# Strassen-Winograd on quarters for the token gating of a fused attention, token-mixing and gating kernel

## The chip, the cores and the metric

One core of a Trainium2 chip. The time is device microseconds of one execution of the whole program, from its first to its last instruction and what lies around them. The kernel before was run three times.

## The reference

Three blocks follow each other, all float32, with B = 2 batches, S = 768 tokens, 8 heads of 64, so D = 512 features:

```python
x = attention(q, k, v)            # near keys of a window, 24 block summaries
theta = x @ w_theta               # 512x512
y = einsum('ts,bsd->btd', w_tok_r, x*cos(theta)) + einsum(..., w_tok_i, x*sin(theta))
u = x + y;  x = u + relu(u @ w_ch)
h = gelu(x @ w_in)                # 512 -> 1024
u, v = h[..., :512], h[..., 512:]
v_n = (v - mean) / sqrt(var + 1e-6) * g_ln
v_s = einsum('ts,bsd->btd', w_sg, v_n) + b_sg[None, :, None]   # token gating, 768x768 by 768x512
out = x + (u * v_s) @ w_out
```

The change is about the line `v_s`: for each batch a product of w_sg (768 x 768) with the normalized v (768 x 512).

## The kernel before

**Number format.** Each float32 product is three matmuls of rounded halves (`mm3`, L347): both operands are split into a high half (a copy to fp32r, on ACT or POOL, `copy`, L337 and L339) and a low half (source minus high, on DVE or POOL, `diff`, L345); TensorE then adds high by high (L350), high by low (L351) and low by high (L352) in PSUM. Weights are split too (`unit`, `unit_f32`, `high_low`).

**Stages.** *Attention* (to about 82 us): pairs of heads, loads k, vT, q, v; scores S, their maximum m and P = S - m on DVE (L640, L646), exp on ACT (L654), transposes PT, copies Pt (ACT or DVE), O, the norm x = O/sum on DVE (L684 to L688), transposes X, copies xT. *Mixing*: theta (th), kk and rr (its turns), f (cos and sin on ACT, L771 and L772, times x), z (split f), y and ys (the two mixing products with w_r, w_i, w_ri). *ch*: u and u @ w_ch. *in_v* (L879): iv groups of 12 matmuls of 512 columns, gelu to vf, statistics st (BN_STATS and aggregate, L902), then for the batch the root (L908), reciprocal rv (L910), six norms (L925), and the splits vh, vl into vn. *in_u* (L945): iu groups, gelu to ut. *sg* (L966): for each batch, four blocks of 128 features by two pieces of tokens (512 and 256): 6 tiles of tokens x 3 matmuls with the split v_n as stationary operand and the split w_sg as moving operand; then the gate (x g_ln + b_sg, DVE, L984), times u (L996), and the split of the result into g for the next product. *outp* (L1016): 12 matmuls for each of 4 blocks of features and 3 blocks of 512 tokens (the last one in two of 256), evacuation with + x on DVE (L1034), store (L1042).

**What sets the order.** The program describes each step as an `op` with its engines, estimated durations, predecessors, buffers, and a key; a list scheduler in the file (`Order`, `play`, L143) picks by key and fixes the order of every engine, of SP's DMA issues too, before the program is built. The tables PLAN, LEAD and SHIFT are numbers that shift these keys. At run time each engine works through its list in that order; SP is one queue for all DMAs. Buffers are slots: 27 W (1024 columns), 19 H (512), 4 X (1536), 6 PSUM banks B and one double bank S. The main order of the keys behind the mixing:

```python
for step, k in ((ch, 0), (ch, 1), (ch, 2), (in_v, 0), (in_u, 0), (in_u, 1), (sg, 0), (in_v, 1),
                (in_u, 2), (outp, 0), (sg, 1), (outp, 1), (outp, 2)):
```

w_sg comes as nine units (`unit_f32`, L473): load, high, low, kept in W slots until sg of batch 1.

## Time and profile before

| what | value |
|---|---|
| runs | 381.68, 382.77, 384.49 us (median 382.77) |
| the profiled execution | 382.36 us |
| its span, first to last instruction | 379.8 us |
| mean granted TensorE clock | 1.000 |
| busy: PE, weight loads, DVE, ACT, POOL | 372.7, 314.9, 241.0, 179.8, 87.5 us |
| matmuls | 2983 |
| DMA | 40.84 MB |

Busy is the time in which an engine had an instruction under way; a matmul's end is modelled, and neighbours overlap, so its step is read from two starts in the timeline. A releaser is what ended an idle time. An idle engine that is not the bound costs nothing.

### The profile page before, as it was taken

The page shows a single profiled execution, that of the slowest core. Times are in us where ns is not written, and L with a number is a line of the kernel's source. Part 1 is how long each engine was busy: PE and PEld are TensorE (multiplying, and loading weights), DVE is VectorE, ACT ScalarE, POOL GpSimd, SP SyncE. Part 2 cuts the span into 40 slices and gives each one's busy share as a digit, 9 for nine tenths or more (in the row PEclk, how much of TensorE's full clock was granted, in tenths as well). Part 3 has the DMA queues.
Part 4 walks back from the last instruction along what each step waited for, and adds up shares of the span by engine and source line. Part 5 has one row for each costly group of instructions (what it writes and reads, how often), then busy time and mean ns, then how long its engine had stood idle before and what let it go on. Part 6 is the DMA issues. An engine that isn't in the chain of part 4 may idle for free.

```text
span 379.8 us, 7439 instructions
## 1 busy us (share of the span) xinstructions
PE 372.7 (98%) x2983; PEld 314.9 (83%) x2983; DVE 241.0 (63%) x418; ACT 179.8 (47%) x321; POOL 87.5 (23%) x113
## 2 busy tenths in 40 slices
PE   8899999999999999999999999999999999999996
PEld 4787887888888888888888888888888889889885
DVE  4999998978786746337869557370344485246422
ACT  2787899969764832225657226362311351012100
POOL 6556546464400200003304403000000030000000
PEclk9999999999999999999999999999999999999999
DMA  8999899980040000013696010010000000200022
GB/s 269 347 361 285 281 296 333 315 286 1 3 151 14 2 0 2 0 28 115 217 340 217 13 44 0 0 36 7 0 2 0 1 2 28 85 0 0 29 93 100
DMA packets 18257, 40.84 MB, mean 108 GB/s; under 512 B 2416, under 2 KB 8752, under 8 KB 18224
## 3 DMA queue, kind: packets, MB, share of 16 engines
q1 hardware_dynamic: 18224, 40.38, 32.0%
q8 instruction: 23, 0.38, 0.4%
q14 instruction: 10, 0.08, 0.1%
HBM read 36.92 MB, written 3.15 MB: 106 GB/s over the span
## 4 chain that ended last, share of the span: by engine, by line
PE 92%; DMA 3%; DVE 2%; issue 1%; SPq 1%; ACT 0%; DVEq 0%
PE y L350 6%; PE y L351 6%; PE y L352 6%; PE sg L351 4%; PE sg L350 4%; PE sg L352 4%; PE ys L351 3%; DMA k<-in_kT_dram 3%; PE ys L352 3%; PE ys L350 3%; PE th L350 3%; PE ch L350 3%; PE ch L351 3%; PE iu L351 3%; PE iu L350 3%; PE iv L351 3%
## 5 line engine op out<-in xcount | busy, mean ns | idle before, releaser
L337 ACT ACTIVATE g<-gf 128x256 fp32r<-128x256 f32 (+1 forms) x20 | 9.1, 462 | 50.8 <-DVE gf L996 43.1
L345 DVE TENSOR_TENSOR z<-f,z 128x512 fp32r<-128x512 f32 x20 | 14.3, 715 | 21.9 <-ACT z L337 19.9
L352 PE MATMUL ys<-w_ri,z 128*128 128x256 f32 x96 | 27.1, 282 | 0.0
L351 PE MATMUL ys<-w_ri,z 128*128 128x256 f32 x96 | 27.1, 282 | 0.0
L350 PE MATMUL ys<-w_ri,z 128*128 128x256 f32 x96 | 26.7, 278 | 0.0
L337 ACT ACTIVATE z<-f 128x512 fp32r<-128x512 f32 x20 | 12.6, 630 | 27.7 <-PE ys L352 19.9
L902 DVE BATCH_NORM_STATS2 st<-vf 128x6 f32<-128x512 f32 x12 | 8.3, 693 | 25.1 <-ACT vf L893 25.1
L350 PEld LDWEIGHTS ys<-w_ri,z 128*128 128x128 f32 x96 | 18.0, 188 | 4.4
L351 PEld LDWEIGHTS ys<-w_ri,z 128*128 128x128 f32 x96 | 18.0, 188 | 3.8
L984 DVE SCALAR_TENSOR_TENSOR gf<-sg,g_sb,bsg 128x512 f32<-128x512 f32 (+1 forms) x16 | 9.9, 617 | 16.8 <-PE sg L352 16.7
L350 PE MATMUL th<-w_th,xh 128*128 128x512 f32 x48 | 19.8, 413 | 0.0
L350 PE MATMUL y<-w_i,z 128*128 128x512 f32 x48 | 19.3, 401 | 0.0
L350 PE MATMUL y<-w_r,z 128*128 128x512 f32 x48 | 19.2, 401 | 0.0
L351 PE MATMUL y<-w_r,z 128*128 128x512 f32 x48 | 19.1, 397 | 0.0
L351 PE MATMUL y<-w_i,z 128*128 128x512 f32 x48 | 19.0, 395 | 0.0
L352 PE MATMUL th<-w_th,xh 128*128 128x512 f32 x48 | 18.8, 392 | 0.0
L351 PE MATMUL th<-w_th,xh 128*128 128x512 f32 x48 | 18.8, 391 | 0.0
L350 PE MATMUL ch<-u,w_ch 128*128 128x512 f32 x48 | 18.7, 390 | 0.0
L351 PE MATMUL ch<-u,w_ch 128*128 128x512 f32 x48 | 18.7, 390 | 0.0
L352 PE MATMUL y<-w_r,z 128*128 128x512 f32 x48 | 18.7, 389 | 0.0
L352 PE MATMUL y<-w_i,z 128*128 128x512 f32 x48 | 18.7, 389 | 0.0
L352 PE MATMUL ch<-u,w_ch 128*128 128x512 f32 x48 | 18.7, 389 | 0.0
(294 smaller groups left out, 1133.1 us busy)
## 6 DMA issues: line engine op xcount, KB each, us to landing
v<-in_vW_dram SPq DMA_DIRECT2D x16, 193.5 KB, 5.3
k<-in_kT_dram SPq DMA_DIRECT2D x8, 384.0 KB, 5.0
q<-in_qT_dram SPq DMA_DIRECT2D x16, 192.0 KB, 5.4
vT<-in_vT_dram SPq DMA_DIRECT2D x8, 384.0 KB, 5.6
w_r<-in_w_rT_dram SPq DMA_DIRECT2D x6, 511.8 KB, 5.9
w_i<-in_w_iT_dram SPq DMA_DIRECT2D x6, 511.8 KB, 6.9
w_th<-in_w_theta_dram SPq DMA_DIRECT2D x4, 511.8 KB, 6.1
w_ch<-in_w_ch_dram SPq DMA_DIRECT2D x4, 511.8 KB, 4.4
```

The source lines that it names most:

```text
L337: ACT.activation(dst, src, AF.Copy, scale=scale)
L345: EN[e].tensor_tensor(out=lo, in0=src, in1=hi.bitcast(F32), op=ALU.subtract)
L350: PE.matmul(ps, ah, bh, start=first, stop=False, skip_group_check=True)
L351: PE.matmul(ps, ah, bl, start=False, stop=False, skip_group_check=True)
L352: PE.matmul(ps, al, bh, start=False, stop=last, skip_group_check=True)
L902: DVE.bn_stats(out=st, in_=T(f"vf{b}_{i}")[:])
L984: DVE.scalar_tensor_tensor(out=T(gn)[:, :n], in0=T(bk)[:, :n], scalar=g_sb[:, f:f + 1], in1=T("bsg")[:, o:o + n], op0=ALU.mult, op1=ALU.add)
```

## The change

The token gating of a batch is now done by Strassen and Winograd's seven products of quarters. Token and feature halves give quarters A11, A12, A21, A22 of the normalized v (3 tiles of 128 tokens by 256 features each) and B11 to B22 of w_sg (3 tiles by 384 columns). `values` makes the sums of A for both batches (four adds of 768 columns, Qa, Qt) and splits seven operands (Qh, Ql, each 768 wide). `weights` does the same for each of three tiles of w_sg: four loads (Qw, 128 x 384), four sums (Qb), seven splits (Qy..h, Qy..l, 384 wide); these are written to a DRAM scratch (dQx, op Qz, two writes of 192 KB) and later read back (Qx, 384 KB) and copied in place on ACT or POOL. `sg` runs products 1, 6, 2, 7, 5, 3, 4, each for two batches and two blocks of features: 9 matmuls of 384 columns in a bank Qs. Product 2 adds into product 1's bank and 3 into 5's; the other sums (U, R) are made by ACT (product 1's copy) and DVE (Qe). Then Qn (gate), Qm (times u), Qg and Qk (split) for 16 blocks of 384 tokens. The norm of v is its own step (`ln`) and runs on ACT or DVE. The output goes in blocks of 384 tokens, the last one in two of 192. The numbers in PLAN and LEAD are new and SHIFT holds an offset for almost every op, so that the order of all engines differs from the start. TensorE's sg matmuls go from 144 of 512 and 144 of 256 columns to 252 of 384; the output's from 132 of 512 and 24 of 256 to 180 of 384 and 24 of 192; filler matmuls (L410) from 13 to 9. Table loads on ACT go from 9 to 13. DMA instructions go from 139 to 208 rows.

```diff
-    at0=-2.908, at0_pair=5.41, at0_half=1.015, at1=29.379, at1_pair=12.053, at1_half=-11.199,
+    q_from=121.281, q_step=28.693, q_back=223.53, at0=-10.9, at0_pair=7.346, at0_half=2.395,
...
+    dr = ctx.enter_context(tc.tile_pool(name="dr", bufs=1, space=bass.MemoryType.DRAM))
...
-    for c in range(NT):
-        unit_f32(("sg", c), [rows(w_sgT, c)[:, :512]], 170 + 3 * c)
-    for c in range(3):
-        unit_f32(("sgs", c), [rows(w_sgT, 2 * c + i)[:, 512:] for i in range(2)], 190 + 3 * c)
...
+            op(f"vo{b}_{i}", {"ACT": act(512), "DVE": 0.54}, norm, after=[f"rv{b}"], use=[vx],
...
+        l1 = hl(1, "A11", n0, [x0])
+        add("c", "t", "A11", "A21", True, n0, [x0], [(t, "W")])
+        add("b", "A11", "A22", "t", True, [l1, f"Qa{b}c"] + n1, [x0, x1, t])
+        hl(6, "A11", [f"Qa{b}b"], [x0])
+        l2 = hl(2, "A12", n1, [x1])
+        add("d", "A12", "A12", "A11", True, [l2, f"Qa{b}b"], [x0, x1])
+        hl(7, "t", [f"Qa{b}c"], [t])
+        add("a", "A21", "A21", "A22", False, n1 + [f"Qa{b}c"], [x0, x1])
+        hl(5, "A21", [f"Qa{b}a"], [x0])
+        hl(3, "A12", [f"Qa{b}d"], [x1])
+        hl(4, "A22", n1, [x1])
...
+            def aside(e):
+                made["d" + nm] = dr.tile([P, QS], F32, tag="d" + nm, name="d" + nm)
+                for i, y in enumerate((h, l)):
+                    nc.sync.dma_start(made["d" + nm][:, sl(i, 384)], T(y)[:, :384].bitcast(F32))
+            op(f"Qz{k}{p}", {"SP": 0.86}, aside, after=[l], use=[h, l], size=2 * moved(P, 1536), parts=2)
+            op(nm, {"SP": 0.43},
+               lambda e: nc.sync.dma_start(T(nm, F32R)[:, :QS].bitcast(F32), made["d" + nm][:]),
+               after=[f"Qz{k}{p}"], new=[(nm, "W")], size=moved(P, 3072), early=PLAN["q_back"],
+               spare=PLAN["q_spare"])
+            op(nm + "l", copies(QS, ("ACT", "POOL")),
+               lambda e: copy(e, T(nm, F32R)[:, :QS], T(nm)[:, :QS].bitcast(F32)), after=[nm],
+               use=[nm], port=("POOL",))
...
+        for p in (1, 6, 2, 7, 5, 3, 4):
+            for b in range(B):
+                for j in range(2):
...
+                    def mm(e, bk=bk, c0=c0, start=start, h=h, l=l, ws=ws, j=j):
+                        for k in range(3):
+                            s = slice(256 * k + 128 * j, 256 * k + 128 * j + 128)
+                            w = T(ws[k], F32R)
+                            mm3(T(bk)[:, c0:c0 + 384], (T(h, F32R)[:, s], T(l, F32R)[:, s]),
+                                (w[:, :384], w[:, 384:768]), start and k == 0, k == 2)
...
-    for step, k in ((ch, 0), (ch, 1), (ch, 2), (in_v, 0), (in_u, 0), (in_u, 1), (sg, 0), (in_v, 1),
-                    (in_u, 2), (outp, 0), (sg, 1), (outp, 1), (outp, 2)):
+    for step, k in ((ch, 0), (ch, 1), (ch, 2), (in_v, range(4)), (in_u, 0), (in_v, range(4, 8)), (in_u, 1),
+                    (in_v, range(8, 12)), (in_u, 2)):
         t = step(k, t)
+    for b in range(B):
+        ln(b)
+    t = sg(t)
+    for k in ((0, 1), (1, 1), (0, 0), (1, 0)):
+        t = outp(k, t)
```

**Order, DVE, end of in_v of batch 1.** Lines of the changed file lie 300 to 460 higher. Before, from the last statistics on:

```order
L902 BN_STATS st1_5_3610<-vf1_5_3606 128x6
L903 BN_AGGR mv1_3406<-st1_5_3610 128x2
L910 RECIPROCAL rs1_3407<-rs1_3407 128x6
L925 TENSOR_SCALAR vf1_0_3404<-vf1_0_3404,mv1_3406,rs1_3407 128x512
L925 TENSOR_SCALAR vf1_1_3431<-vf1_1_3431,mv1_3406,rs1_3407 128x512
```

In the changed kernel (Ql11 is the low half of operand 1 of batch 1, Qt1 a difference of quarters, Ql07 batch 0's):

```order
L1191 BN_STATS st1_5_3685<-vx1_1_3607 128x6
L1192 BN_AGGR mv1_3483<-st1_5_3685 128x2
L1205 RECIPROCAL rs1_3484<-rs1_3484 128x6
L1206 SCALAR_TENSOR_TENSOR rs1_3484<-mv1_3483,rs1_3484 128x6
L1218 TENSOR_SCALAR vx1_0_3478<-vx1_0_3478,mv1_3483,rs1_3484 128x512 x3
L1261 TENSOR_TENSOR Qt1_3722<-vx1_0_3478 128x768
L645 TENSOR_TENSOR Ql11_3746<-vx1_0_3478,Qh11_3728 128x768
L1261 TENSOR_TENSOR vx1_0_3478<-vx1_1_3607,Qt1_3722 128x3x256
L645 TENSOR_TENSOR Ql07_3762<-Qt0_3480,Qh07_3732 128x768
```

Three of the six norms moved to ACT, and sums of quarters and their low halves stand where the plain splits stood; Ql11 is the low half that product 1 of batch 1 reads.

**Order, ACT, attention stage.** Before (one pair of table loads up to here; kk, f: theta's turns and the sine, P: exp):

```order
L763 ACTIVATE f0_0_1293<-rr0_1283 128x256
L337 ACTIVATE Pt5_0_0_1301<-PT5_0_0_1287 120x384
L337 ACTIVATE Pt5_0_1_1313<-PT5_0_1_1297 120x384
L771 ACT_TABLE_LOAD
L771 ACTIVATE f0_0_1293<-f0_0_1293,half_pi_134 128x256
L772 ACTIVATE f0_0_1293<-rr0_1283 128x256
L654 ACT_TABLE_LOAD
L654 ACTIVATE P6_1_1321<-P6_1_1321 128x720
```

In the changed kernel:

```order
L1054 ACT_TABLE_LOAD
L1054 ACTIVATE f0_0_1042<-f0_0_1042,half_pi_136 128x256
L1055 ACTIVATE f0_0_1042<-rr0_1024 128x256
L937 ACT_TABLE_LOAD
L937 ACTIVATE P4_1_1064<-P4_1_1064 128x720
L1026 ACTIVATE kk2_1141<-th2_1050 128x512
L1046 ACTIVATE f1_0_1147<-rr1_1054 128x256
L1054 ACT_TABLE_LOAD
L1054 ACTIVATE f1_0_1147<-f1_0_1147,half_pi_136 128x256
L1055 ACTIVATE f1_0_1147<-rr1_1054 128x256
```

f of tile 0 has moved ahead by some ten rows, f of tile 1 stands two rows behind P of the next pair, and each return to P is a further table load.

**Order, SP, loads of w_in.** Before (w_inu, w_inv: the halves of w_in; w_sg..r: the raw gating weights):

```order
L448 DMA w_inu0_2664<-in_w_in_dram 128x2047
L479 DMA w_sg3r_2689<-in_w_sgT_dram 128x512
L448 DMA w_inu1_2708<-in_w_in_dram 128x2047
L479 DMA w_sg4r_2713<-in_w_sgT_dram 128x512
L479 DMA w_sg5r_2743<-in_w_sgT_dram 128x512
L448 DMA w_inu2_2753<-in_w_in_dram 128x2047
L448 DMA w_inu3_2757<-in_w_in_dram 128x2047
L448 DMA w_inv0_2784<-in_w_in_dram 128x2047
L448 DMA w_inv1_2795<-in_w_in_dram 128x2047
```

In the changed kernel:

```order
L1321 DMA dQx12_2746<-Qy12h_2713 128x384
L1321 DMA dQx12_2746<-Qy12l_2732 128x384
L1321 DMA dQx23_2793<-Qy23h_2721 128x384
L1321 DMA dQx23_2793<-Qy23l_2790 128x384
L1294 DMA Qw200_2803<-in_w_sgT_dram 128x384
L1294 DMA Qw210_2828<-in_w_sgT_dram 128x384
L1321 DMA dQx21_2841<-Qy21h_2830 128x384
L1321 DMA dQx21_2841<-Qy21l_2838 128x384
L1321 DMA dQx22_2864<-Qy22h_2859 128x384
L1321 DMA dQx22_2864<-Qy22l_2862 128x384
L748 DMA w_inu2_2887<-in_w_in_dram 128x2047
L748 DMA w_inv2_2890<-in_w_in_dram 128x2047
```

The loads of the gating weights now carry writes of their splits with them, each behind a split by ACT, DVE or POOL, and these stand ahead of w_inu2 and w_inv2; three earlier w_inu loads and four more pairs of writes stand above this piece.

## Rows read from the trace of the kernel before

**Rows 1.** The page: busy time of each engine, last chain, one group of weight loads.

```profile
PE 372.7 (98%) x2983; PEld 314.9 (83%) x2983; DVE 241.0 (63%) x418; ACT 179.8 (47%) x321; POOL 87.5 (23%) x113
...
PE 92%; DMA 3%; DVE 2%; issue 1%; SPq 1%; ACT 0%; DVEq 0%
...
L350 PEld LDWEIGHTS ys<-w_ri,z 128*128 128x128 f32 x96 | 18.0, 188 | 4.4
```

**Rows 2.** Windows of 20 us: us, busy us (instructions) by engine, PEclk, DMA share, GB/s.

```profile
0.00:20.00 20.00, 17.45 (x375) 12.14 (x375) 14.09 (x25) 10.40 (x17) 12.90 (x35) 1.00 0.94 308
20.00:40.00 20.00, 18.87 (x426) 15.78 (x423) 19.18 (x35) 16.25 (x29) 10.65 (x15) 1.00 0.97 316
40.00:60.00 20.00, 20.00 (x410) 16.74 (x403) 19.03 (x39) 18.40 (x33) 12.07 (x18) 1.00 0.92 301
60.00:80.00 20.00, 19.55 (x258) 16.37 (x258) 15.48 (x29) 17.71 (x33) 12.21 (x11) 1.00 0.97 323
...
100.00:120.00 20.00, 20.00 (x107) 17.15 (x106) 14.81 (x23) 14.12 (x28) 3.05 (x2) 1.00 0.22 79
...
200.00:220.00 20.00, 20.00 (x90) 16.49 (x89) 15.98 (x28) 9.77 (x16) 7.55 (x5) 1.00 0.38 120
...
300.00:320.00 20.00, 20.00 (x118) 17.78 (x117) 12.88 (x24) 8.06 (x13) 3.48 (x4) 1.00 0.04 14
```

**Rows 3.** Timeline of PE: start us, duration us, engine, line, operation.

```profile
335.62 0.39 PE L352 MATMUL sg<-w_sg,vn 128*128 128x512 f32 x1
...
340.83 0.39 PE L351 MATMUL sg<-w_sg,vn 128*128 128x512 f32 x1
...
346.05 0.28 PE L350 MATMUL sg<-w_sgs,vn 128*128 128x256 f32 x1
...
354.56 0.28 PE L352 MATMUL sg<-w_sgs,vn 128*128 128x256 f32 x1
...
376.50 0.28 PE L352 MATMUL o_3b<-g,w_out 128*128 128x256 f32 x1
```

**Rows 4.** Instructions by form, PE, 195 to 380 us: xcount | busy us, mean ns.

```profile
L350 PE MATMUL sg<-w_sg,vn 128*128 128x512 f32 x48 | 18.7, 389 | 0.0
...
L350 PE MATMUL o<-g,w_out 128*128 128x512 f32 x44 | 17.1, 390 | 0.0
...
L350 PE MATMUL sg<-w_sgs,vn 128*128 128x256 f32 x48 | 13.6, 283 | 0.0
```

**Rows 5.** One line of DVE (ns min/median/max, first and last start), then instructions by form.

```profile
L688 DVE TENSOR_TENSOR x<-O,ri x16: 557/558/558, 15.9 to 81.6; 128x384 f32<-128x384 f32 x16
...
L345 DVE TENSOR_TENSOR w_ch<-w_ch3r,w_ch 128x512 fp32r<-128x512 f32 x1 | 1.8, 1796 | 0.0
...
L432 DVE SCALAR_TENSOR_TENSOR w_th<-w_th1r,w_th 128x512 fp32r<-128x512 f32 x1 | 0.7, 693 | 0.0
```

**Rows 6.** Instructions by form, ACT.

```profile
L337 ACT ACTIVATE Pt<-PT 120x384 f32<-120x384 f32 x26 | 11.5, 490 | 5.0 <-PE PT L659 4.8
...
L337 ACT ACTIVATE v<-ones 24x774 f32<-24x774 f32 x10 | 8.5, 851 | 0.3
...
L908 ACT ACT_TABLE_LOAD x2 | 2.6, 1283 | 0.0
```

**Rows 7.** Instructions by form, POOL.

```profile
L345 POOL TENSOR_TENSOR xh<-xT,xh 128x384 fp32r<-128x384 f32 x8 | 8.1, 1010 | 1.5 <-ACT xh L337 1.4
```

**Rows 8.** Timeline of ACT around the square root of batch 1.

```profile
302.84 1.28 ACT L908 ACT_TABLE_LOAD   x1
304.14 0.30 ACT L908 ACTIVATE rs<-mv,eps_t 128x6 f32<-128x6 f32 x1
304.98 1.28 ACT L957 ACT_TABLE_LOAD   x1 [0.54 <-issue]
```

**Rows 9.** DMA issues: xcount, KB each, median us to landing.

```profile
k<-in_kT_dram SPq DMA_DIRECT2D x8, 384.0 KB, 5.0
```

**Rows 10.** Timeline of DVE, the last output piece.

```profile
376.82 0.42 DVE L1034 TENSOR_TENSOR o_3bs<-o_3b,xT 128x256 f32<-128x256 f32 x1 [1.01 <-PE o_3b L352]
```

## The prediction

> **What bounds the kernel now.** I read the busy times and the chain that ended last first [rows 1]. TensorE is busy 372.7 of 379.8 us and the chain is 92% TensorE; DVE has 63%, ACT 47%, POOL 23%. Then the stretches of 20 us [rows 2]: from 80 to 360 us every stretch, those not shown too, reads 20.00 for PE, so no joint between stages costs anything there. TensorE has holes only in the attention stage: 17.45, 18.87, 20.00 and 19.55 of 20 up to 80 us, where DVE has 19.18 and 19.03 in the second and third and the DMA share is 0.92 to 0.97. [...] So a matmul saved behind 80 us is worth its whole step, as long as the other engines keep feeding PE, and work added to DVE or ACT before 80 us can cost.

> A matmul's step is the distance of two starts: its busy time (389 or 283 ns, [rows 4]) has a modelled end and overlaps the next. Of 24 sg matmuls of 512 columns in a row the first starts at 335.62 and the last at 340.83: 5.21/23 = 0.2265 us each (by groups of 12, 2.72, I use 0.2267). Of 72 with 256 columns the first starts at 346.05 and the last at 354.56: 8.51/71 = 0.1199 [rows 3]. The line through both has 0.1068 us for 256 columns more, so 0.1733 us for 384 columns and 0.0933 for 192.

> **The change part by part.** Products: sg was 144 matmuls of 512 and 144 of 256 columns [rows 4], 144 x (0.2267 + 0.1199) = 49.9 us. Now it is 7 products x 4 (two batches, two halves of features) x 9 = 252 of 384 columns, 252 x 0.1733 = 43.7 us: **-6.2 us**. An eighth of the columns goes; a little is given back since the fixed part of a step is paid on shorter ones.

> Output: 132 x 0.2267 + 24 x 0.1199 = 32.8 us becomes 180 x 0.1733 + 24 x 0.0933 = 33.4 us: **+0.7 us**. Both are behind 80 us, where PE is the bound: **-5.5 us**.

> The step of 384 is interpolated. A 256-column step of 0.12 is already shorter than the busy time of a weight load (188 ns, [rows 1]), so loads overlap and don't set the step. [...]

> Weights: seven splits of each of 3 k-tiles come in place of nine f32 units. That is 12 sums and 21 high and 21 low halves of 384 columns, spread over 100 to 290 us, where DVE has 4 to 15 us idle in every 20, ACT 6 to 15 and POOL 12 to 19 (the fullest, 100:120 and 200:220, are shown [rows 2]). By 558 ns for a 384-wide DVE instruction, 490 ns on ACT and 1010 ns for a POOL difference [rows 5 to 7], it is some 30 us over three engines: hidden. The scratch is 42 writes of 192 KB and 21 reads of 384 KB, 16 MB; DMA's share is 0 to 0.38 in every stretch of 100 to 180 and 200 to 320, so the bytes are hidden. What is not free is order: SP issues one after another, and the write of a low half that is not ready holds the loads behind it. In the order, w_inu's last tile and all of w_inv stand behind eight such pairs. By adding durations, PE asks for that w_inu tile some 3.5 us later than it can be there. Nothing, then; without that cover each us is paid one to one.

> Normalization of batch 1: before, sg of batch 1 began long after its statistics, with sg of batch 0 and o0 between. Now the first product needs it at once. After the last iv group PE has only three iu groups of 2.72 and the two batch-0 halves of product 1 (18 x 0.1733 = 3.12), 11.3 us. The chain in that time: gelu, BN_STATS and aggregate, table load 1.28, sqrt 0.30, reciprocal [rows 8], three norms of 0.6, Qt's difference 0.95, table load back, two gelus, Qh11's 768-wide copy 0.85, Ql11's difference 0.95. The last gelu waits for the third iu group, so the chain's end is fixed by PE itself. An evacuation starts 0.32 us behind the last matmul's start (376.50 and 376.82, [rows 3, 10]), 0.42 for 512 columns; then 0.60, 0.85 and 0.95 make 2.8 us. The third matmul of batch 1, which first uses Ql11, starts 0.23 + 3.12 + 0.35 = 3.7 us behind it. Hand-offs take some of the 0.9 left; I take **+0.2 us** for a row ahead in line that is late, with 0 and 2 as bounds.

> Within sg: DVE has some 65 instructions, 37.5 of 44 us; ACT about 25, POOL about 20. Product by product the feeding halves have 1.5 to 6 us of slack. Nothing, in the likely case.

> Attention stage: the new numbers move every engine's order from the start. Up to the last norm (L688; last at 81.6 us, [rows 5]) DVE has 4.5 us more: two Pt copies 1.1, two xh splits 2.1, one vs reduce 0.94, one f product 0.7 and one more weight sum 0.7, less one z difference 0.7 and a small copy. ACT has four more table loads (1.283 us each [rows 6]; 13 in place of 9 in the whole kernel) and 9.1 us more up to the last Pt copy, 66.3 in place of 57.2. Against this, four of thirteen filler matmuls are gone, and 1.05 us of mixing leaves the stretch. Bounds: -1 us (fewer holes), +4.5 us (all of DVE's extra is paid, since 19 of 20 us are busy at 20 to 60). I take **+1.0 us**: nearer the low end, as PE itself has only 1.6 us of holes between 20 and 80 us [rows 2] and DVE 6.3 us. [...]

> Tail: the last block is 192 columns, its evacuation 0.15 us shorter than the 0.42 of [rows 10]: -0.1 at most, left out.

> **Sum:** the profiled execution took 382.36 us (span 379.8 and 2.6 around it): 382.4 - 5.5 + 0.2 + 1.0 = **378.0 us**. It lies 0.4 below the median of 382.77, well inside the runs' 381.7 to 384.5.

> **Rivals.** *A: the helpers bind in sg, no change.* POOL has two- and one-input work of 20 us beside DVE's 37.5, and DVE is 85% full. With POOL beside it, a 512-wide DVE difference went from 693 to 1796 ns [rows 5]. If ten of DVE's two-input instructions meet POOL at +1.1 us, 11 us go into 6.5 us of room: 4.5 us of waiting products, 382.5. For it: these rows, and that POOL had only 0 to 3.5 us of work per 20 from 260 us on. Against: POOL's tasks there number 20, some while DVE reads PSUM. [...]

> *B: the attention stage gives most of it back.* If DVE's 4.5 us is paid whole: 378.0 - 1.0 + 4.5 = 381.5, no change. For: DVE 19 of 20 us. Against: PE can take theta and mixing groups meanwhile, and their sum is the same.

> *C: the read-back comes late, slower.* A product needs three reads of 384 KB into W slots and three copies in place. A 384 KB load took 5.0 us to landing [rows 9], and the next two are on the queue behind it, by 300 GB/s another 1.3 us each; with the 0.85 us copy, 8.5 us from a slot that comes free, while one product covers 36 x 0.1733 = 6.2 us. If slots come free only one product ahead, each of five later products waits 2.2 us: 378.0 + 11 = 389. It decides where fewer than one and a half products' slots (five of the 27) are free ahead. For: SP's order has the last 17 reads in a run, most of them behind a wait for PE, and ACT copies nearly all. Against: w_inu and w_inv leave eight slots as sg starts. A fall of the clock would add to it; none shows before.

> *D: a 384-column step is not between its neighbours* but bound by loads, 0.188: 252 x 0.188 + 180 x 0.188 + 2.2 = 83.4 against 82.7 us before: 384.5 with the rest, no change. Against it: the 0.12 step.

> **How the numbers follow.** About 1% is what a measurement of this kernel can tell from no change: 378.9 to 386.6. Chances: forecast 0.55 (374.5 to 380.5, four fifths of it below 378.9 as the attention term is the only wide one), A 0.15, B 0.15, C 0.12, D 0.03. Faster: 0.55 x 0.8 + some of A and B = 0.50; slower: C and part of A = 0.14; the rest 0.36. The range takes in the bounds (382.4 - 5.5 - 1 - an unmodelled 1 below; A, B and half of what is between them and C above): 374.5 to 386.

> **What would show it.** Right: matmuls of sg start 0.173 apart, 252 of them; PE at 20.00 in all stretches from 85 us on; the last L688 norm (L971 there) by about 83 us; PE idle under 0.5 us before the batch-1 half of product 1. Wrong: PE idle before Qs groups with DVE (A) or ACT's copies of Qx and the DMA of Qx (C) as releaser; PE holes over 5 us before 85 us (B); a step of 0.18 or more (D); the granted clock under 1.00.

## The result: 0.99 of the time before

The changed kernel took 380.84 us (median of 20 runs), the kernel before 384.40 beside it: ratio 0.9906, 95% interval 0.9882 to 0.993. The ratio leaves out the few runs far above the rest (383.99 and 928.91 us of the changed kernel, 2096.41 of the kernel before). The forecast was 378.0 with 374.5 to 386. The profiled execution took 380.85 us with a span of 379.1; that of before 382.36 with 379.8. So the two traces explain 1.5 us, 0.7 in the span and 0.8 around it. The medians differ by 3.6: the profiled execution of before is one of its short ones.

The page of the changed kernel has the busy times, the last chain, one group of the products, and the queue that carries instructions:

```profile
PE 369.4 (97%) x2991; PEld 321.9 (85%) x2991; DVE 261.6 (69%) x453; ACT 204.1 (54%) x349; POOL 120.1 (32%) x145
...
q8 instruction: 23, 0.38, 0.4%
...
PE 82%; DMA 5%; DVE 5%; ACT 3%; issue 2%; POOL 1%; SPq 1%; POOLq 0%; DVEq 0%; ACTq 0%
...
L650 PE MATMUL Qs<-Qx,Qh 128*128 128x384 f32 x84 | 28.2, 336 | 0.2 <-DVE U L1458 0.2
...
L637 ACT ACTIVATE Qx<-Qx 128x768 fp32r<-128x768 f32 x20 | 16.6, 843 | 9.3 <-DMA Qx<-dQx 6.4
```

Against [rows 1] TensorE is busy 3.3 us less, DVE 21, ACT 24 and POOL 33 us more. The Qs line is a third of the products, the 84 high by high matmuls, with 0.2 us of idle PE ahead of them; the page has 0.0 for the other two thirds. ACT waited 6.4 us for the read-back, PE did not.

The stretches of 20 us, with the columns of [rows 2]:

```profile
0.00:20.00 20.00, 16.89 (x349) 11.97 (x350) 13.81 (x22) 8.63 (x14) 13.56 (x36) 1.00 0.93 303
20.00:40.00 20.00, 17.73 (x334) 15.24 (x333) 16.64 (x33) 15.87 (x30) 9.78 (x12) 0.91 0.97 316
40.00:60.00 20.00, 19.81 (x329) 16.28 (x328) 19.64 (x35) 16.62 (x27) 13.92 (x20) 1.00 0.92 295
60.00:80.00 20.00, 19.78 (x420) 17.11 (x419) 18.81 (x38) 17.99 (x30) 12.41 (x13) 1.00 0.85 271
80.00:100.00 20.00, 19.56 (x119) 15.99 (x118) 19.16 (x31) 15.24 (x27) 8.00 (x7) 1.00 0.36 132
...
300.00:320.00 20.00, 19.78 (x115) 19.46 (x114) 13.92 (x21) 13.14 (x20) 8.78 (x7) 1.00 0.39 135
320.00:340.00 20.00, 20.00 (x117) 20.00 (x117) 15.52 (x32) 8.66 (x12) 9.19 (x9) 1.00 0.33 107
```

From 100 to 300 us and from 320 to 360 PE is full. The forecast had that from 85 us on; there it is idle for 0.16 us between 90 and 95 and for 0.22 near 308.9. From 20 to 40 us much more is missing: 17.73 of 20 against 18.87 before, and the granted clock of that stretch is 0.91. Finer windows and the timeline show what stands there:

```profile
30.00:32.00 2.00, 0.75 (x24) 0.49 (x21) 1.76 (x4) 2.00 (x4) 1.50 (x2) 1.00 1.03 306
32.00:34.00 2.00, 1.54 (x39) 1.50 (x39) 1.05 (x2) 0.28 (x1) 1.06 (x1) 0.85 1.01 347
34.00:36.00 2.00, 2.00 (x7) 1.68 (x6) 1.93 (x6) 1.40 (x4) 0.00 (x0) 0.50 0.95 310
36.00:38.00 2.00, 2.00 (x29) 1.50 (x28) 0.51 (x1) 1.35 (x4) 0.00 (x0) 0.79 0.80 260
```

```profile
30.25 0.50 PE L890 MATMUL S<-k,q 64*64 64x96 f32 x14
32.46 0.41 PE L890 MATMUL S<-k,q 64*64 64x96 f32 x9 [1.72 <-issue]
...
34.79 0.63 PE L651 MATMUL th<-w_th,xh 128*128 128x512 f32 x1
35.21 0.63 PE L652 MATMUL th<-w_th,xh 128*128 128x512 f32 x1
```

In the middle of a group of 24 equal matmuls, 14 run, PE stands still for 1.72 us and the other 10 follow. The releaser is "issue": PE waited for nothing that the profile shows. Then, from 33.4 to 36.8 us, the clock is 0.50: theta's 512-column matmuls start 0.42 us apart in place of 0.2267. The waits of PE put this first of all (the third, left out here, is for the warm-up data and is 1.3 us before and after):

```profile
PE S L890 <- issue: 1.7, 1, 1.7
PE S L881 <- DVE P L929: 1.3, 4, 0.4
...
PE PT L942 <- ACT P L937: 0.6, 1, 0.6
PE vp L846 <- POOL vs L842: 0.5, 1, 0.5
```

By the starts of PE's matmuls the span divides like this (counted from both traces, us):

```
                                     before   after    forecast
all ahead of products and output     293.87   297.61   +1.0 and +0.2
products                              49.90    44.21   -6.2
output, with the last step            32.85    33.87   +0.7
```

So three sizes are off: +3.7 for +1.2, -5.7 for -6.2, and +1.0 for +0.7. The sum is -0.9; the end behind the last matmul is 0.2 longer.

### The profile page after: what moved, and what is told of

The parts are those of the page before. It is cut to its first block, busy times and chain, and to the rows that moved or that the text cites. A ratio compares the mean times of both kernels' runs of the same rounds, so it can differ in the third digit from the quotient of the medians.

```text
span 379.1 us, 7679 instructions
## 1 busy us (share of the span) xinstructions
PE 369.4 (97%) x2991; PEld 321.9 (85%) x2991; DVE 261.6 (69%) x453; ACT 204.1 (54%) x349; POOL 120.1 (32%) x145
## 4 chain that ended last, share of the span: by engine, by line
PE 82%; DMA 5%; DVE 5%; ACT 3%; issue 2%; POOL 1%; SPq 1%; POOLq 0%; DVEq 0%; ACTq 0%
PE y L650 6%; PE y L651 6%; PE y L652 6%; PE Qs L650 3%; PE Qs L651 3%; PE Qs L652 3%; PE ch L650 3%; PE ys L651 3%; PE ch L651 3%; PE ys L652 3%; PE iu L652 3%; PE iu L651 3%; PE ch L652 3%; PE iu L650 3%; PE iv L652 3%; PE iv L651 3%
## 5 line engine op out<-in xcount | busy, mean ns | idle before, releaser
L650 PE MATMUL Qs<-Qx,Qh 128*128 128x384 f32 x84 | 28.2, 336 | 0.2 <-DVE U L1458 0.2
L652 PE MATMUL Qs<-Qx,Ql 128*128 128x384 f32 x84 | 28.1, 334 | 0.0
L651 PE MATMUL Qs<-Qx,Qh 128*128 128x384 f32 x84 | 28.1, 334 | 0.0
L637 ACT ACTIVATE Qx<-Qx 128x768 fp32r<-128x768 f32 x20 | 16.6, 843 | 9.3 <-DMA Qx<-dQx 6.4
L650 PE MATMUL th<-w_th,xh 128*128 128x512 f32 x48 | 20.6, 428 | 0.2 <-DVE xT L642 0.2
L1061 DVE TENSOR_TENSOR f<-f,x 128x512 f32<-128x512 f32 x21 | 16.0, 763 | 5.4 <-ACT f L1055 5.1
L652 PE MATMUL th<-w_th,xh 128*128 128x512 f32 x48 | 19.3, 402 | 0.3 <-DVE xh L645 0.3
L650 PE MATMUL y<-w_i,z 128*128 128x512 f32 x48 | 19.3, 402 | 0.0
L651 PE MATMUL th<-w_th,xh 128*128 128x512 f32 x48 | 19.3, 401 | 0.0
L650 PE MATMUL y<-w_r,z 128*128 128x512 f32 x48 | 19.2, 399 | 0.0
L651 PE MATMUL y<-w_r,z 128*128 128x512 f32 x48 | 19.0, 397 | 0.0
L651 PE MATMUL y<-w_i,z 128*128 128x512 f32 x48 | 19.0, 395 | 0.0
L645 DVE TENSOR_TENSOR Ql<-vx,Qh 128x768 fp32r<-128x768 f32 x10 | 9.4, 960 | 13.7 <-PE iu L652 9.4
L650 PE MATMUL ch<-u,w_ch 128*128 128x512 f32 x48 | 18.8, 392 | 0.0
L650 PE MATMUL iu<-tx,w_inu 128*128 128x512 f32 x48 | 18.7, 390 | 0.0
```

What stands on the lines that cost most here:

```text
L637: ACT.activation(dst, src, AF.Copy, scale=scale)
L645: EN[e].tensor_tensor(out=lo, in0=src, in1=hi.bitcast(F32), op=ALU.subtract)
L650: PE.matmul(ps, ah, bh, start=first, stop=False, skip_group_check=True)
L651: PE.matmul(ps, ah, bl, start=False, stop=False, skip_group_check=True)
L652: PE.matmul(ps, al, bh, start=False, stop=last, skip_group_check=True)
L1061: EN[e].tensor_tensor(out=z3(), in0=z3(), in1=x.unsqueeze(1).to_broadcast([P, 2, 256]), op=ALU.mult)
```

## The experiments

Each trace was read in the same way for PE's list: all PE rows (weight loads, matmuls, semaphore and drain rows) in the order of their starts, counted from 0. In the trace of the changed kernel the row behind the 1.72 us, in a score group (S), has position 1217, and 1217 = 193 + 4 x 256 (the 193 is read off the stops, which all lie at 193 plus a multiple of 256). The profile's instruction queue moves blocks of 0.38 MB / 23 = 16.5 KB. This is the ground of theory S below: a stop at a block's edge of the instruction list, not at a place of the program. Steps over an edge are given from start to start, idle time is shorter. Its rivals, together theory D in the expectations, are the new order itself (rival B of the prediction) and helpers that feed PE late (A and C).

**1. The same kernel again.**

> The changed kernel once more, beside the three others of this series. [...] Theory S (the stop): the stop is there in every run and the fall of the clock in about two of three; ratio to before 0.990 with single times from 378 to 382. Theory D (DVE and ACT have more to do before the last norm): the attention stage is late in every run by the same amount, about 3.7 us against before.

380.33 us median of 6 runs (378.89 to 380.94) to 384.43: 0.988 [0.984, 0.992]. The stop is at position 1217 again, now with 0.84 us of idle time (1.08 from start to start, 32.19 to 33.27 us), and the clock's fall lies elsewhere, at 11.2 to 14.7 us, behind a wait of 1.7 us for POOL (vp, at 10.38). The place repeats, its length does not. Nor does the fall come in two runs of three, as expected: one of these 6 has a mean granted clock under 0.999.

**2. The list shifted by 40 entries.** Two long warm-up matmuls give way to 22 short ones; PE's later rows and all other engines' lists are the changed kernel's.

```diff
-                PE.matmul(ps[:], warm[:, :P], warm[:, P:640], start=True, stop=True)
+                w = 512 if j < 3 else 32
+                PE.matmul(ps[:, :w], warm[:, :P], warm[:, P:P + w], start=True, stop=True)
-    op("fill", {"PE": 2.25}, filler(5), after=["warm0"], use=["warm"], new=[("warmb", "B")], key=-100)
+    op("fill", {"PE": 2.25}, filler(25), after=["warm0"], use=["warm"], new=[("warmb", "B")], key=-100)
```

> The first warm-up of PE has 25 matmuls (3 of 512, 22 of 32 columns) in place of 5 of 512, so that all that follows stands 40 entries later in PE's list; the lists of the other engines and all data are as in the changed kernel. Theory S: the stop follows the place in the list, so position 1217 is now 4 entries ahead of that score group, where PE waits for DVE anyway; the stop of 1.7 us and the fall of the clock (another 1.7) go: 377.5 us, ratio 0.982, last norm of attention at about 82.5 us in place of 86.0. Theory D: nothing changes: ratio 0.990, last norm at 86.

381.23 us (9 runs), 0.9916 [0.988, 0.9952]. The waits and the timeline of PE:

```profile
PE O L958 <- issue: 2.8, 1, 2.8
```

```profile
29.60 0.94 PE L958 MATMUL O<-v,Pt 120*64 120x65 f32 x22
33.31 0.28 PE L958 MATMUL O<-v,Pt 120*64 120x65 f32 x2 [2.76 <-issue]
```

The S group of before runs without a stop; the stop stands 40 entries earlier in the program, between two O matmuls, and is again position 1217. So the place in the list decides, not the program. The hope that it would vanish was wrong: it was 1 us longer, and the clock's fall followed at 34.8. The time alone would fit theory D; the moved stop doesn't.

**3. The order of before for attention and mixing, the rest of the change kept** (PLAN and LEAD of before and no SHIFT for those ops; the numbers of all later ops kept).

```diff
-    q_from=121.281, q_step=28.693, q_back=223.53, at0=-10.9, at0_pair=7.346, at0_half=2.395,
+    q_from=121.281, q_step=28.693, q_back=223.53, at0=-2.908, at0_pair=5.41, at0_half=1.015,
...
```

> The seven products, the scratch and the output of 384 as in the changed kernel, but the attention and mixing stages in the order of the kernel before (its numbers for these stages; the first 1000 rows of PE's list and the first 160 of ACT's and DVE's are the same as before). Theory D: the 3.7 us of the attention stage come back: 377.1 us, ratio 0.981, last norm at 82. Theory S: the same stop as in the kernel before (0.5 us, no fall of the clock) in place of 1.7 + 1.7 us: the gain is about 3 us in runs where the clock falls, 1.2 in others: 378, ratio 0.983. Either way the last norm stands at 82 and the 4.8 us of products and output remain; if the ratio stays at 0.990, the attention stage isn't what took the rest of the gain.

387.01 us (12 runs), 1.0068 [1.0042, 1.0094]. Both theories had expected 377 to 378. The products start at 295.87, 1.7 us earlier than in the profiled run of the change and hardly earlier than with the new order in load_more (5 and 6 below, 295.96); against the 293.87 of before that is 2.0 later, and position 1217 stops here too (1.46 us from start to start, 0.70 before). The last norm stands at 82.8, as expected, and ahead of the products PE waits 1.9 us for other engines, against 3.0 in the changed kernel. The loss lies behind it: the products take 47.94 us in place of 44.21 and the output 38.1 in place of 33.9, and the windows and waits say why.

```profile
320.00:340.00 20.00, 18.29 (x106) 17.97 (x105) 14.93 (x31) 8.33 (x13) 8.27 (x9) 1.00 0.38 132
340.00:360.00 20.00, 17.35 (x90) 16.74 (x89) 18.02 (x37) 5.32 (x10) 1.02 (x1) 0.91 0.11 39
```

```profile
PE o L482 <- DVE w_out L475: 2.3, 1, 2.3
PE Qs L480 <- ACT Qx L467: 2.1, 2, 1.7
...
PE Qs L480 <- DVE U L1288: 0.7, 1, 0.7
```

This is rivals A and C come true in another order: PE waits for ACT's copy of a read-back, for DVE, for a split of w_out, and the clock falls at 346.8 to 350.2. The scheduler orders all that follows anew, so the order behind the mixing differs too (u @ w_ch runs from 197.3 to 233.1 us here, from 187.7 to 240.3 in the changed kernel). So this run shows that the products' margin hangs on the order, but not on which part of it, and it doesn't isolate the order of the attention stage.

**4. The kernel before, shifted by 40 in the same way** (the edit of 2).

> Control: the kernel before with the same 40 entries more ahead in PE's list. Theory S: its own stops (0.70, 0.42 and 0.46 us between starts at positions 1217, 2497 and 2753) move to other places, 1177, 2457 and 2713 of the old list; the time changes by up to 1.5 us either way, 383 to 385. Theory D: no change, 384.4, ratio 1.000 within 0.002.

386.12 us (12 runs), 1.0049 [1.0016, 1.0081]. The stops of before were at positions 1217, 2497 and 2753. Expected was that they stay at these positions, so at other places of the program, and 383 to 385 us; instead they are now at 961 (2.23 us from start to start) and 2241 (0.90), other edges of the list. So which edges stop PE isn't fixed. The kernel before has the same kind of stops; in its profiled execution they were short. The interval lies above 1, if barely.

**5 and 6. Less and more on the DMA queue.** A load of 512 KB (w_r0) goes 11 places later, or a further 512 KB load is put behind it.

```diff
-    for o in order.play():
+    ops = order.play()
+    order.by["w_r0d"].start, order.by["w_r0t"].start = 30.9, 39.5
+    for o in sorted(ops, key=lambda o: o.start):
```

```diff
+        if o.name == "w_r0d":
+            extra = cp.tile([P, 2048], I16, tag="W24", name="extra")
+            nc.sync.dma_start(extra[:, :2047], rows(w_rT, 0)[:, :512].bitcast(I16)[:, 1:])
```

> One load of 512 KB (w_r0, first needed by the mixing) and its conversion on ACT stand later: on SP behind the second q load of pair 4 in place of ahead of w_th2, eleven places. Nothing else moves. Theory S, refined by the four traces so far (PE stops where the next block of 256 list entries has not come, and runs on 2.4 to 2.6 us after the transfer of that block began; the transfer begins late because it stands behind loads in the DMA engines): 512 KB less, 1.6 us at 320 GB/s, stand ahead of the block that is needed at position 1217, so the stop of 1.1 to 2.0 us shrinks to under 0.5 us, the clock stays at 1.00 in most runs, and the time is 378.6 us, ratio 0.985 or lower. Theory D (DVE's and ACT's longer lists set the end of attention): nothing changes, 380.5, ratio 0.989 as with the changed kernel.

> The dose the other way: one load of 512 KB more (a second copy of w_r0's raw data into a free buffer, read by nobody) right behind w_r0's, ahead of w_th2; nothing else moves. Theory S: the block needed at position 1217 comes 1.6 us later, the stop grows from 1.1 to 2.0 us to about 3 us, and the clock falls in every run: 382.3 us, ratio 0.994. Theory D: w_th and the later loads land 1.6 us later, which DVE and ACT meet with their own waits; the stop at 1217 stays as it is and the time grows by 0 to 1 us.

379.85 us (6 runs; 0.9886 [0.9848, 0.9924]) and 379.21 (4 runs; 0.9868 [0.9839, 0.9896]). The intervals overlap with each other and with the changed kernel's. The stop at 1217 is there in both, 1.14 and 1.41 us from start to start. Expected were a stop under 0.5 us and 378.6, and a stop of about 3 us and 382.3. Half a megabyte either way moved neither as theory S had it: no dose shows.

**7 and 8. Shifts by 80 and by 216.** The warm-up as in 2, with 45 matmuls (two of 512 columns) for 80 and 62 (one of 512) for 216; these are the lines for 216, whose last two add 51 short ones to the filler group.

```diff
-                PE.matmul(ps[:], warm[:, :P], warm[:, P:640], start=True, stop=True)
+                w = 512 if j < 1 else 32
+                PE.matmul(ps[:, :w], warm[:, :P], warm[:, P:P + w], start=True, stop=True)
-    op("fill", {"PE": 2.25}, filler(5), after=["warm0"], use=["warm"], new=[("warmb", "B")], key=-100)
+    op("fill", {"PE": 2.25}, filler(62), after=["warm0"], use=["warm"], new=[("warmb", "B")], key=-100)
...
+        for j in range(51 * (n == 9)):
+            PE.matmul(ps[:, :32], identb[:], maskb[:, 0, :32], start=True, stop=True)
```

> PE's list is 80 entries longer ahead of the first real matmul (43 warm-up matmuls of 32 columns in place of three of 512), everything else is the changed kernel's. Position 1217 of PE's list is then the place that the changed kernel has at 1137, reached at about 28.7 us. Theory S1 (the transfer of the block that holds position 1217 cannot start before about 30 us, because of the traffic of that stretch): it starts at 29.8 to 30.7 us as in the four traces so far, PE goes on at 32.2 to 33.3 us, so the stop grows to 3.5 to 4.5 us; about 382. Theory S2 (the transfer starts some 4 to 5 us after PE has passed the boundary before): that boundary is reached at about 23.5 us, the transfer starts near 28.4, PE goes on near 30.9, a stop of about 2 us; about 380.5. Rival (the place in the list has nothing to do with it): no stop at position 1217, the stop stays in the S group at 30.5 to 32.5 us.

> 216 entries more ahead of the first real matmul (57 more warm-up matmuls of 32 columns with four of 512 made 32, and 51 more of 32 columns in the filler group behind the first scores), everything else as in the changed kernel. 216 is 40 short of a block of 256: the boundary that stopped PE at 30.5 us moves 40 entries later in the program, to about 31.5 to 32 us (as position 1473), and the one before it (1217) to about 26 us. Both theories on the transfer's start make the stop near 31.5 us shorter: with a transfer that starts at 30 us (S1) 0.5 to 1 us is left, with one that follows the boundary of 26 us by 4 to 5 us (S2) about the same; the stop at 26 us is the open one: none if its transfer starts by 23.5. If the whole stop and the clock's fall behind it are gone, Qs starts at 294.5 to 295 and the time is 377.5 to 378. Rival (the stops belong to the program's place, not to the list): as the changed kernel, 1 to 2 us at 30.5 us, 379 to 381.

Shifted by 80: 379.94 us (4 runs), 0.9894 [0.9856, 0.9932]; waits on "issue" of 1.2 us at an O group and 1.0 at two S groups. The step over position 1217 is 1.45 us, where the two theories had 3.5 to 4.5 and 2. Shifted by 216: 383.99 us (10 runs), 0.9998 [0.9971, 1.0024], where 377.5 to 381 were expected. The place near 31 us is free and position 1473 stops PE for 0.75 us at 35.8, as expected, but PE also stops at 17 us, with the clock at 0.50 from 21.0 to 24.4, in waits and timeline:

```profile
PE S L893 <- issue: 2.6, 2, 2.0
```

```profile
17.17 0.24 PE L893 MATMUL S<-ks,q 64*64 64x24 f32 x3
19.43 0.54 PE L893 MATMUL S<-ks,q 64*64 64x24 f32 x21 [2.02 <-issue]
```

The edges can now be laid side by side, with the transfer of the block behind each (us from the span's start; "reached" is the start of the last row ahead of the edge, "went on" that of the first behind it):

```
trace           edge   transfer starts  reached  went on   went on - transfer
before          1217   29.43            31.21    31.91     2.48
after           1217   30.07            30.50    32.46     2.39
same            1217   30.67            32.19    33.27     2.60
shift40         1217   30.67            30.32    33.31     2.64
shift80         1217   29.81            31.08    32.52     2.71
shift216         705   16.75            17.20    19.43     2.68
shift216        1217   26.93            30.85    30.89     3.96 (no stop)
hybrid          1217   30.45            31.43    32.90     2.45
before_shift40   961   23.45            23.76    25.99     2.54
load_later      1217   30.07            31.37    32.51     2.44
load_more       1217   29.84            30.88    32.29     2.45
tail96 (9.)     1217   31.61            32.14    34.37     2.76
```

In all eleven traces together there are 110 edges from 705 to 3009. At 24 of them PE stops (a step of over 0.25 us), and goes on 2.39 to 2.83 us after the transfer's start. At none does it go on earlier than 2.28. And all 19 waits of PE of over 0.15 us that the eleven traces put down to "issue" stand at such an edge. Behind 86 us, where one transfer more has gone than edges are passed, no edge stops it. This is shown. What sets the transfer's start is not shown. Both theories of run 7 gave it about right (29.81), because PE passed the edge before at 25.08 and not at 23.5. In run 8 it starts at 26.93, only 1.2 us behind the edge before it (25.75), where shift40 has 6.7: that stands against a fixed delay (S2). Traffic (S1) is not excluded by it, as the DMA share just before was lower than in the changed kernel: 0.69, 0.47 and 0.30 in the three stretches of 2 us from 18 us on, against 1.01 to 1.03.

**9. The last block as 288 + 96 columns** in place of 192 + 192.

```diff
-                                  [slice(0, 192), slice(192, 384)]):
+                                  [slice(0, 288), slice(288, 384)]):
```

> The last block is cut 288 + 96 columns in place of 192 + 192. If a matmul's step has a floor near 0.11 us (the 192-column step measured 0.1096, the line through wider ones says 0.0933), the 96-column step is 0.105 to 0.115 and the two pieces take 12 x 0.1333 + 12 x 0.11 = 2.92 us in place of 2.63, so the end is 0.1 to 0.3 us later (the last evacuation is some 0.1 us shorter). Rival (no floor, 192 was slow for another reason, as the change of bank or of the weights): 96 columns step by 0.053 us, the two take 2.24 us, 0.4 to 0.5 us earlier.

One run, 381.81 us, so the total says little; the starts of the matmuls do. The timeline at the 96-column piece:

```profile
371.39 0.21 PE L650 MATMUL o_3b<-g,w_out 128*128 128x96 f32 x1
371.43 0.28 PE L651 MATMUL o_3b<-g,w_out 128*128 128x96 f32 x1
371.54 0.27 PE L652 MATMUL o_3b<-g,w_out 128*128 128x96 f32 x1
371.65 0.27 PE L650 MATMUL o_3b<-g,w_out 128*128 128x96 f32 x1
...
372.66 0.40 PE L650 MATMUL o<-g,w_out 128*128 128x384 f32 x1
...
374.83 0.29 PE L650 MATMUL o_3a<-g,w_out 128*128 128x288 f32 x1
...
376.28 0.29 PE L652 MATMUL o_3a<-gx,w_out 128*128 128x288 f32 x1
```

The second to the fourth start 0.11 apart; the 12 take 371.39 to 372.66, 0.106 each. With 192 columns it was 0.1096 (12 from 370.94 to 372.26 in the changed kernel); the 288-column ones step by 1.45 / 11 = 0.132. So there is a floor of about 0.11 us, as expected (by the line through the steps of 256 and 384 it is reached near 230 columns, an estimate), and the two pieces take longer, not shorter: the output is 0.26 us longer.

## Why the prediction came out right, step by step

**The sum** was right by sizes that partly cancelled, so in part by luck. (By its own figures the output term is 33.4 - 32.8 = 0.6, not 0.7, the terms as written add up to 378.1, not 378.0, and rival D's to 384.3, not 384.5.) Against the 382.77 that the prediction had for before, the measured ratio stands for 379.2 us: inside the band of its forecast (374.5 to 380.5), but 0.3 beyond the 378.9 up to which it would have called the change faster. What the runs allow is a comparison without the clock's falls: of 24 runs of the changed kernel, 12 had a mean granted clock of 0.999 or 1.000, and their median is 379.6 us; the other 12 (0.991 to 0.998) have 381.6. Of 50 runs of before beside the experiments, 44 had the full clock, median 384.1, and 6 had not, 385.7. At the full clock the change is worth 4.6 us; the sum said 4.4. But only 4.1 of the 4.6 are in the span (381.85 and 377.75, medians of the same runs), the rest lies around it, where the sum had put nothing. About 2 us go in half of the runs with a fall of the clock; in the profiled execution it lasted 3.41 us.

**Products, -6.2: a size off by 0.5.** The interpolated step is right: of the timeline lines below, those at 339.75 and 341.65 are 11 steps apart, 0.173 each. The 0.5 is one place, at the eighth group of nine matmuls (timelines of PE, DVE and POOL):

```profile
308.38 0.34 PE L652 MATMUL Qs<-Qx,Ql 128*128 128x384 f32 x1
308.93 0.44 PE L650 MATMUL Qs<-Qx,Qh 128*128 128x384 f32 x1 [0.22 <-DVE U L1458]
309.21 0.34 PE L651 MATMUL Qs<-Qx,Qh 128*128 128x384 f32 x1
...
339.75 0.33 PE L650 MATMUL Qs<-Qx,Qh 128*128 128x384 f32 x1
...
341.65 0.33 PE L652 MATMUL Qs<-Qx,Ql 128*128 128x384 f32 x1
...
370.94 0.25 PE L650 MATMUL o_3b<-g,w_out 128*128 128x192 f32 x1
371.03 0.28 PE L651 MATMUL o_3b<-g,w_out 128*128 128x192 f32 x1
371.14 0.27 PE L652 MATMUL o_3b<-g,w_out 128*128 128x192 f32 x1
371.26 0.27 PE L650 MATMUL o_3b<-g,w_out 128*128 128x192 f32 x1
```

```profile
303.76 0.95 DVE L645 TENSOR_TENSOR Ql<-Qt,Qh 128x768 fp32r<-128x768 f32 x1
304.62 1.58 DVE L1261 TENSOR_TENSOR vx<-vx,vx 128x768 f32<-128x768 f32 x1
306.13 1.81 DVE L645 TENSOR_TENSOR Ql<-vx,Qh 128x768 fp32r<-128x768 f32 x2
307.87 1.47 DVE L1458 TENSOR_TENSOR U<-Qs,U 128x384 f32<-128x384 f32 x3
```

```profile
303.99 1.41 POOL L639 TENSOR_SCALAR Qh<-vx 128x768 fp32r<-128x768 f32 x1 [6.65 <-PE Qs L651]
```

A DVE sum of 768 columns takes 0.96 us; the one at 304.62, while POOL copies Qh until 305.40, took 1.58. Two splits stand behind it, and by the order of DVE the evacuation that PE waits for comes some 0.6 us later (no run took the overlap away): two steps of 0.55 and 0.28 us in place of 0.173. That is rival A, at 0.5 us and in one place where it had asked for ten. (The two rows from which A's price was taken are no clean pair: POOL worked beside the 693 ns one too, a copy from 30.04 to 31.06 us; beside the 1796 ns one it made differences.) Why the sum is longer beside POOL was not shown; the trace has the 0.6 us.

**Normalization of batch 1, +0.2: it was 0.** The first product starts at 297.61, its batch-0 half takes 18 steps, and the batch-1 half follows at 300.75 without a gap. The step's bound (under 0.5 us) holds.

**Output, +0.7: about +1.0.** The 384-column step is 0.1733 as interpolated. The 192-column step was taken as 0.0933 from a line through wider ones and is 0.1096 by the lines above, 24 x 0.016 = 0.4 us. The step that failed is the extension of the line below 256 columns: something holds the step up at 192 that doesn't at 256. There the argument used against rival D ("loads overlap and don't set the step", from the 256-column step) is open too: the steps of 106 ns at 96 and 110 ns at 192 columns are nearly the same, as a floor makes them, and the 188 ns that the profile shows as a load's busy time do not stand between two starts. Whether the load sets the floor was not shown: no run changed its width. It is no floor of every matmul: the warm-up matmuls of shift216 (32 columns in bfloat16, each with a load of 128) step by 0.027 us. The trace of before had a warning: the transposes X, of 128 columns in float32, start 0.109 us apart, where the line gives 0.067.

**Attention stage, +1.0: it was +3.7 in the profiled execution.** This is the term that failed in size. Without a fall of the clock it is still +2.1 to +4.2: the products start at 295.96 in load_more, 296.24 in load_later, 297.53 in shift80 and 298.07 in tail96, against 293.87. The term counted work on DVE and ACT, and the last norm came at 86.0 against the 83 of the prediction:

```profile
L971 DVE TENSOR_TENSOR x<-O,ri x16: 556/558/558, 16.0 to 86.0; 128x384 f32<-128x384 f32 x16
```

The work was not hidden: PE's waits of over 0.15 us for other engines ahead of the products, without the one for the warm-up, come to 3.0 us after and 1.6 before, so +1.5 where the term had +1.0; in all eight traces with the new order they are 2.8 to 3.9. (Two waits at edge 705 that the traces of load_later and tail96 put down to ACT are counted with the edges below.) Lines of before, to be set beside those of the result:

```profile
PE S L598 <- DVE P L646: 1.0, 3, 0.4
PE S L607 <- issue: 0.7, 2, 0.5
...
PE O L674 <- issue: 0.2, 1, 0.2
```

What the term lacked is what PE's own list does: waits on "issue" at the edges of 1.7 us, 0.9 before, so +0.8 (1.1 to 3.2 us at the edges in the eight traces), and the clock at 0.50 for 3.41 us behind the stop (half of it, +1.7). The three make 4.0, 0.3 more than measured; shorter gaps and the four fillers fewer are not in them. Two of the prediction's signs of being wrong came true: the clock under 1.00, and PE holes of over 5 us before 85 us (6.1, but 4.1 before the change). Rival B's size came about by its own cause only in part.

**Scratch and weights, nothing: right.** Not one matmul of the products waited for a read-back (rival C), though ACT did for 6.4 us; hybrid's 2.1 us shows that the margin hangs on the order.

**What lies around the span** was taken as unchanged at 2.6 us. It is 1.75 to 1.84 in the runs of the changed kernel and 2.1 to 2.6 in those of before: -0.6 us that no step had. Hybrid and tail96 have 1.8 as well, so neither the order of the attention stage nor the cut of the last block makes it; its cause stays open. So does why the profiled execution of before was 1.8 us under the median of its full-clock runs.

## What to carry to other kernels

Where a stage consists of many small matmuls, look in PE's waits for "issue" in the middle of a uniform group, and count the rows to it: if such stops lie multiples of 256 apart, as all 19 here do, it is the list. Here three shifts of the list only moved them, and one load later or more changed nothing that the runs can tell. Add up what PE waits for, by cause, over the whole stage before and after, and not at one place alone. Where fewer columns per matmul are to save work, measure the step at the narrowest piece before the line is extended: here it stayed at 0.106 and 0.110 us at 96 and 192 columns, where the line had 0.053 and 0.093. And compare an order tuned for one plan with another only as a whole: the old order put back for two stages cost 6 us.

## What the runs showed of the hardware that was not expected

Five of the eleven traces have a fall of the granted clock to 0.50, for 3.41 us, while PE still has work. Each stands behind a time in which PE stood still: at an edge of its list for 1.7 to 2.8 us in after, shift40 and shift216 (the fall comes 0.9 to 1.6 us after PE went on), in a wait of 1.7 us for POOL in same and of 2.3 us for DVE in hybrid (0.9 and 0.1 us after). So the fall doesn't belong to the list's stops alone. It is no rule either: PE stood still for 2.0 us in tail96 and in before_shift40 and for 1.7 us in hybrid (near 337 us), and the clock stayed at 1.00. Why, stays open. Each fall costs about 1.7 us where PE is the bound (half of 3.41; an estimate).
